# A third buffer for the split probabilities, and the magnitude sums written into the second query tile

## The chip, the cores and the metric

The program runs on one core of one Trainium2 chip. Its engines work side by side, each through its own queue in order: TensorE (PE, with its weight loads as PEld), VectorE (DVE), ScalarE (ACT), GpSimd (POOL) and SyncE (SP), which here issues nearly all DMAs. The metric is the device time of one execution in microseconds (us); less is better.

## The reference

Three parts follow one another. Inputs and output are float32.

```
scores = q @ k.T / sqrt(64)               # 4 batches x 8 heads, 576 tokens, 64 wide
kth    = 32nd largest of each row
attn   = softmax(where(scores >= kth, scores, -1e9))
x      = (attn @ v)                       # as 2304 tokens x 512
h      = x @ w_in;  x = softplus(h) @ w_out               # 512 -> 2048 -> 512
expert = argmax(x @ w_gate)               # 8 experts, one for each token
out    = gate * (relu(x @ w1[expert]) @ w2[expert])       # 512 -> 1024 -> 512
```

## The kernel before, in words

**Pairs.** Two heads of a batch make a pair; there are 16 (`m` = 0 to 15), four for each batch. For a pair, `prep_load` loads q, k and v into the raw tiles `qn`, `kn`, `vn` (pool `raw`, one buffer each, so that the next pair's load waits until this pair's tile has been read). `prep_split` cuts each number into two float16 halves: ACT writes the high half (lines 362 and 375), POOL the rest (363, 376; DVE for the first pair). Transposing DMAs bring k into `kt` (line 365) and q into `q1` (368), two plain DMAs copy q1 with its halves changed into `q2` (369, 370), and v goes to `v16`. The pool `kv`, which holds q1, q2, kt and v16, has four buffers: pair m writes where pair m-4 was.

**Magnitude sums.** `magnitudes` lets ACT take the absolute values of qn, kn and vn and keep only the sums of the rows, which a later check reads; the values themselves go to a scratch tile (`junk`, pool `stg`, one buffer) that nobody reads. For the first pair it is called at the end of `prep_split`, for the others at the end of `prep_load`.

**Groups.** The score tiles go in 72 groups of two. For a group, PE makes the scores in two pieces (line 401), which ACT copies from PSUM (lines 411 and 447). DVE finds the 32 largest of each row (lines 441 to 467). Then for both tiles ACT applies the threshold (477), POOL subtracts (478), ACT takes the exponential (479). Last, ACT writes the high half of the probabilities into `p16` (line 487), POOL the rest in two pieces (488, 489), and SP issues a DMA that transposes p16 into `pT` (491). The pool `row` gives p16 two buffers, so that the copy of line 487 waits for the transpose of the second tile before it. `e` has three buffers, pT six. The products with v (506, 508) follow three groups later. The trace gives p16 as `p`.

**The rest.** When all groups of a tile of tokens are done, it becomes a part of a unit of 256 tokens for the first layer pair (`layer1` at line 593, `layer2` at 633); the steps are emitted between the groups, 1.7 for each. After a unit come the gate and the place of each token (`route`), the row is written (698), and POOL issues an indirect DMA that scatters the tokens' numbers into a table in DRAM (701). Units 9 and 10 run behind the attention, and from about 861 us on the experts of `part_two` (lines 894 to 978).

**Order.** The program is written as a sequence with priorities. A planner puts it in order for each engine by estimated times and by when a buffer is free; on the chip each engine then runs its list in order and waits at semaphores. The branch in which `flags` is None repeats the work in another way when the check fails; with these inputs it isn't run.

Of the kernel before, what the change touches and what calls it, by code (L numbers as in the profile page):

```python
# [10 lines left out]
F16 = mybir.dt.float16  # L11
# [8 lines left out]
B, H, S, D = 4, 8, 576, 64  # L20
NT, DM, DFF = 2304, 512, 2048
E, F2 = 8, 1024
R = 9
# [38 lines left out]
LATEJ = 1  # L62
DVS = 1
C = 512
LAG = 3
SCALE = 1
ZFILL = 1
LATE = ((2, 8), (3, 0))
# [128 lines left out]
def part_one(tc, ctx, q, k, v, w_in, w_out, const, ident, before, ones, iota_e, reg_e, wg, ids,  # L197
# [8 lines left out]
    row = pool("row", 2)  # L206
    raw = pool("raw", RB)
    stg = pool("stg", 1)
# [107 lines left out]
    def prep_load(m):  # L316
        b, hp = pairs[m]
        src = []
        bd = sm.tile([128, 3], F32, name="bd") if flags is None else sums[:, m]
        for i, x in enumerate((q, k, v)):  # L320
            t = raw.tile([128, R * D], F32, name="qkv"[i] + "n")
            nc.sync.dma_start(t, x[b, 2 * hp:2 * hp + 2].rearrange("h (p r) d -> (h p) (r d)", r=R))
            src.append(t)
        pair[m] = (src, bd)
        if flags is None or m >= LATEJ:
            magnitudes(m)

    def magnitudes(m):
        src, bd = pair[m]
        junk = stg.tile([128, R * D], F16, name="junk")  # L330
        for i, t in enumerate(src):
            nc.scalar.activation(junk, t, AF.Abs, accum_out=bd[:, i:i + 1])

# [16 lines left out]
    def prep_split(m):  # L350
        qn, kn, vn, sc = pair[m] if flags is None else (*pair[m][0], None)
        sub = nc.vector if m < DVS else nc.gpsimd
        q1 = kv.tile([128, 2, R, D], F16, name="q1")
        q2 = kv.tile([128, 2, R, D], F16, name="q2")
        kt = kv.tile([128, R, 128], F16, name="kt")
        for i, xs in enumerate((kn, qn)):
            xv = xs.rearrange("p (r d) -> p r d", d=D)
            if i and m < ST0:
                st = row.tile([128, R, 2, D], F16, name="p16")
            else:  # L360
                st = stg.tile([128, R, 2, D], F16, name="st")
            nc.scalar.activation(st[:, :, 0, :], xv, AF.Copy)
            sub.tensor_tensor(out=st[:, :, 1, :], in0=xv, in1=st[:, :, 0, :], op=ALU.subtract)
            if i == 0:
                nc.sync.dma_start_transpose(out=kt, in_=st.rearrange("p r s d -> p (r s d)"))
            else:
                for h in range(2):
                    nc.sync.dma_start_transpose(out=q1[:, h], in_=st[64 * h:64 * h + 64].rearrange("p r s d -> p (r s d)"))
        nc.sync.dma_start(q2[0:64], q1[64:128])
        nc.sync.dma_start(q2[64:128], q1[0:64])  # L370

        v16 = kv.tile([128, 2, 5, 2 * D + 2], F16, name="v16")
        vs = stg.tile([128, R, 2 * D + 2], F16, name="vs")
        xv = vn.rearrange("p (r d) -> p r d", d=D)
        nc.scalar.activation(vs[:, :, 0:D], xv, AF.Copy)
        sub.tensor_tensor(out=vs[:, :, D + 2:], in0=xv, in1=vs[:, :, 0:D], op=ALU.subtract)
        nc.gpsimd.memset(vs[:, :, D:D + 2], 1.0)
        for h in range(2):
            src = vs[64 * h:64 * h + 64]
            nc.sync.dma_start(v16[0:64, h], src[:, 0:R:2])  # L380
            nc.sync.dma_start(v16[64:128, h, 0:4], src[:, 1:R:2])
            nc.sync.dma_start(v16[64:128, h, 4], src[:, 8])
        if flags is not None and m < LATEJ:
            magnitudes(m)
        pair[m] = (q1, q2, kt, v16, sc)

    sc_t, pt_t, o_t, x_t = {}, {}, {}, {}
# [31 lines left out]
    def emit_softmax(gi):  # L419
        group = groups[gi]  # L420
        n = range(2)
        s2, ps = sc_t.pop(gi)
        s = [s2[:, i] for i in n]
        sc = [pair[g[0]][4] for g in group]
        flb = 1 if flags is None else FLB
        if gi % flb == 0:
            tops[0] = sm.tile([128, 2 * flb, 32], F32, name="mx", bufs=2)
        mx = tops[0][:, 2 * (gi % flb):2 * (gi % flb) + 2]
        kth = mx[:, :, 31:32]
        e = [row.tile([128, S], F32, name="e", bufs=3) for _ in n]  # L430
        bt = sm.tile([128, 2, 1], F32, name="bias")
        if flags is None:
            src = list(s)
            wk = [row.tile([128, S], F32, name="wk") for _ in n]
        else:


            gl = ps[:, :, PS + US:PS + US + QS]
            gh = row.tile([128, 2, QS], F32, name="gt", bufs=1)
            w2 = row.tile([128, 2, S], F32, name="wk", bufs=WKB)  # L440
            nc.vector.tensor_tensor(out=gl, in0=ps[:, :, :QS], in1=s2[:, :, :QS], op=ALU.max)  # L441
            nc.vector.tensor_tensor(out=gh, in0=ps[:, :, QS:PS], in1=s2[:, :, QS:PS], op=ALU.max)
            nc.vector.tensor_tensor(out=w2[:, :, :QS], in0=gl, in1=gh, op=ALU.max)
            nc.vector.tensor_tensor(out=w2[:, :, QS:PS], in0=gl, in1=gh, op=ALU.min)
            nc.vector.tensor_copy(w2[:, :, PS:PS + US], ps[:, :, PS:PS + US])
            nc.vector.tensor_tensor(out=w2[:, :, PS + US:], in0=ps[:, :, :PS], in1=s2[:, :, :PS], op=ALU.min)
            nc.scalar.activation(s2[:, :, PS:], ps[:, :, :PS + US], AF.Copy)  # L447
            src = [w2[:, i, :QS] for i in n]
            wide = (QS, QS, PS + US, S)
        for i in n:  # L450
            nc.vector.max(out=mx[:, i, 0:8], in_=src[i])
        if flags is not None:
            nc.scalar.activation(bt, mx[:, :, 0:1], AF.Copy, scale=-SCORE, bias=LN_ESC)
        else:
            for i in n:
                nc.vector.tensor_scalar(bt[:, i], mx[:, i, 0:1], sc[i][:, 4:5], LN_ESC, op0=ALU.mult, op1=ALU.add)
        if flags is None:
            for i in n:
                nc.scalar.activation(e[i], s[i], AF.Exp, bias=bt[:, i], scale=sc[i][:, 3:4])
        for j in range(3):  # L460
            for i in n:
                to = wk[i] if flags is None else src[i]
                nc.vector.match_replace(out=to, in_to_replace=mx[:, i, 8 * j:8 * j + 8], in_values=src[i],  # L463
                                        imm_value=NEG)
                src[i] = to if flags is None else w2[:, i, :wide[j + 1]]
            for i in n:
                nc.vector.max(out=mx[:, i, 8 * j + 8:8 * j + 16], in_=src[i])  # L467
        if flags is not None and gi % FLB == FLB - 1:
            g0 = 2 * (gi - FLB + 1)
            nc.vector.tensor_tensor(out=flags[:, g0:g0 + 2 * FLB],  # L470
                                    in0=tops[0][:, :, 31:32].to_broadcast([128, 2 * FLB, 2]),
                                    in1=tops[0][:, :, 15:24:8], op=ALU.is_gt)
        for i in n:
            if flags is not None:
                if i == 0:
                    nc.scalar.activation(kths[:, 2 * gi:2 * gi + 2], kth, AF.Copy, scale=K_UP)
                nc.scalar.activation(e[i], s[i], AF.Relu, bias=kths[:, 2 * gi + i], scale=-K_UP)  # L477
                nc.gpsimd.tensor_tensor(out=e[i], in0=s[i], in1=e[i], op=ALU.subtract)  # L478
                nc.scalar.activation(e[i], e[i], AF.Exp, bias=bt[:, i], scale=SCORE)  # L479
                continue  # L480
            mk = row.tile([128, S], F16, name="mk")
            nc.vector.tensor_scalar(mk, s[i], kth[:, i], None, op0=ALU.is_ge)
            nc.gpsimd.tensor_tensor(out=e[i], in0=e[i], in1=mk, op=ALU.mult)
        for i in n:

            p16 = row.tile([128, R, 2, D], F16, name="p16").rearrange("p r s d -> p (r s d)")
            nc.scalar.activation(p16[:, 0:S], e[i], AF.Copy)  # L487
            nc.gpsimd.tensor_tensor(out=p16[:, S:S + D], in0=e[i][:, S - D:], in1=p16[:, S - D:S], op=ALU.subtract)  # L488
            nc.gpsimd.tensor_tensor(out=p16[:, S + D:], in0=e[i][:, 0:S - D], in1=p16[:, 0:S - D], op=ALU.subtract)  # L489
            pT = row.tile([128, R, 128], F16, name="pT", bufs=2 * LAG)  # L490
            nc.sync.dma_start_transpose(out=pT, in_=p16)
            pt_t[group[i]] = pT
# [272 lines left out]
    for b, hp, ts in visits:  # L765
# [3 lines left out]
        m = len(pairs) - 1 - pairs[::-1].index((b, hp))  # L769
# [17 lines left out]
    credit, started = 0, 0  # L787
    for i in range(-1, n + LAG):
        if i == -1:
# [22 lines left out]
        if 0 <= i < n:  # L812
            with tc.high_priority(offset=AHEAD):
                emit_softmax(i)
            with tc.high_priority(offset=0):
                decode_some(DECR)
        j = i - LAG
        if j >= 0:
# [283 lines left out]
```

## Time and profile before

| | us |
|---|---|
| median of 3 runs | 1096.41 (1095.99 to 1100.68) |
| profiled execution, its own time | 1104.11 |
| its span, first to last instruction | 1102.3 |
| PE busy | 900.3 (82% of the span) |
| DVE busy | 852.6 (77%) |
| ACT busy | 833.1 (76%) |
| POOL busy | 603.8 (55%) |

Busy times are sums over the span. The stages differ: attention with the first layer pair up to about 752 us, the last units up to about 861, then the experts. The profiled execution is one execution; its own time stands beside its span because the durations of the rows are those of this execution.

### The profile page before, as it was taken

To read this page: it belongs to the slowest core of one execution; us is meant where nothing else is said; L and a number is where in the kernel's file an instruction comes from. 1 tells how busy PE (TensorE), PEld (TensorE's weight loads), DVE (VectorE), ACT (ScalarE), POOL (GpSimd) and SP (SyncE) were. 2 spreads that over 40 slices of the span, in tenths; PEclk is the share of its full clock that TensorE was granted. 3 is DMA by queue.
4 is the path that set the end of the run, shared out by engine and by line. 5 is a ranking of instruction groups with operands and counts; after the bars stand their busy time and mean duration, and the time that the engine had idled before them with its cause. 6 is when DMAs were issued, how large, how long until landed. Compare 5 with 4: busy or idle time off the path is not lost.

```text
span 1102.3 us, 22261 instructions
## 1 busy us (share of the span) xinstructions
PE 900.3 (82%) x7146; PEld 664.0 (60%) x7146; DVE 852.6 (77%) x2921; ACT 833.1 (76%) x2026; POOL 603.8 (55%) x631
## 2 busy tenths in 40 slices
PE   1124359675978978799989799998999999999995
PEld 0012246344655655666556566666688899999993
DVE  3898999699966847889889799982445897777774
ACT  4889899798868867989897898994478655555553
POOL 2788898798656756767776877773101011211111
PEclk9976569876988989899999999999999999999998
DMA  7888898776756878867978646644601486676660
GB/s 173 202 200 182 180 205 180 164 159 129 126 77 122 143 122 119 134 76 126 139 153 124 106 79 93 86 80 67 202 1 30 99 252 205 217 245 227 228 222 23
DMA packets 295860, 156.98 MB, mean 142 GB/s; under 512 B 257524, under 2 KB 257652, under 8 KB 295732
## 3 DMA queue, kind: packets, MB, share of 16 engines
q1 hardware_dynamic: 292116, 145.73, 63.1%
q0 software_dynamic: 3616, 9.72, 2.6%
q8 instruction: 58, 0.95, 0.4%
q14 instruction: 70, 0.57, 0.2%
HBM read 77.89 MB, written 11.11 MB: 81 GB/s over the span
## 4 chain that ended last, share of the span: by engine, by line
PE 37%; DMA 19%; ACT 17%; POOL 9%; DVE 8%; issue 5%; SPq 3%; POOLq 0%; ACTq 0%; DVEq 0%
PE h L933 9%; DMA pT<-p 9%; PE y L946 9%; PE h L593 6%; PE y L633 4%; POOL p L489 3%; PE y L630 3%; ACT p L487 3%; POOL e L478 2%; DMA w<-in_moe_w_out_dram 2%; ACT e L479 2%; ACT e L477 2%; DVE mx L467 2%; DMA vn<-in_v_dram 2%; DVE wk L463 1%
## 5 line engine op out<-in xcount | busy, mean ns | idle before, releaser
L593 PE MATMUL h<-xT,w_in_s 128*128 128x256 f16 (+1 forms) x1920 | 231.8, 272 | 18.6 <-DMA xT<-xh 7.4
L633 PE MATMUL y<-w_out_s,g 128*128 128x512 f32 x480 | 233.9, 610 | 2.0 <-ACT g L608 2.0
L593 PEld LDWEIGHTS <-w_in_s 128*128 128x128 f16 x1920 | 177.0, 102 | 86.4 <-issue 53.8
L478 POOL TENSOR_TENSOR e<-s,e 128x576 f32<-128x576 f32 x144 | 204.0, 1432 | 22.1 <-ACT e L477 21.8
L467 DVE MAX8 mx<-wk 128x8 f32<-128x128 f32 (+2 forms) x432 | 201.1, 500 | 0.1
L401 PEld LDWEIGHTS <-q 128*128 128x128 f16 (+1 forms) x640 | 56.2, 109 | 195.7 <-issue 148.5
L489 POOL TENSOR_TENSOR p<-e,p 128x512 f16<-128x512 f32 x144 | 167.3, 1162 | 0.0
L463 DVE MATCH_REPLACE8 wk<-mx,wk 128x128 f32<-128x128 f32 (+1 forms) x432 | 144.4, 340 | 0.0
L487 ACT ACTIVATE p<-e 128x576 f16<-128x576 f32 x144 | 97.9, 683 | 42.1 <-DMA pT<-p 41.3
L401 PE MATMUL sa<-kt,q 128*128 128x256 f16 (+1 forms) x320 | 52.9, 304 | 86.7 <-ACT s L411 35.2
L633 PEld LDWEIGHTS y<-w_out_s,g 128*128 128x128 f32 x480 | 83.4, 194 | 62.4 <-issue 57.4
L913 POOL DMA_INDIRECT out_dram<-ot,idx x19 | 19.6, 1030 | 176.3 <-DVE ot L912 156.5
L479 ACT ACTIVATE e<-e,bias 128x576 f32<-128x576 f32 x144 | 111.0, 772 | 6.1 <-POOL e L478 5.9
L401 PE MATMUL sb<-kt,q 128*128 128x320 f16 (+1 forms) x320 | 63.6, 342 | 63.4 <-ACT s L447 63.4
L933 PEld LDWEIGHTS h<-xT,wf 128*128 128x128 f32 x864 | 111.9, 191 | 5.3 <-ACT wf L894 0.2
L933 PE MATMUL h<-xT,wf 128*128 128x256 f32 x864 | 114.0, 283 | 0.0
L946 PE MATMUL y<-wf,hT 128*128 128x512 f32 x432 | 112.9, 399 | 0.3 <-DVE ds L690 0.3
L477 ACT ACTIVATE e<-s,kths 128x576 f32<-128x576 f32 x144 | 106.2, 770 | 1.2 <-POOL p L489 0.4
L506 PE MATMUL m<-v,pT 128*128 128x65 f16 (+1 forms) x1440 | 96.0, 203 | 8.1 <-ACT xtail L534 6.8
L488 POOL TENSOR_TENSOR p<-e,p 128x64 f16<-128x64 f32 x144 | 45.6, 317 | 96.4 <-ACT p L487 80.9
L506 PEld LDWEIGHTS <-pT 128*128 128x128 f16 (+1 forms) x1440 | 89.5, 107 | 14.2 <-issue 10.9
L441 DVE TENSOR_TENSOR sb<-sb,s 128x256 f32<-128x256 f32 x72 | 30.6, 425 | 73.0 <-ACT s L411 48.9
(204 smaller groups left out, 1885.5 us busy)
## 6 DMA issues: line engine op xcount, KB each, us to landing
w1r<-in_moe_w_dram SPq DMA_DIRECT2D x20, 1024.0 KB, 6.0
w2r<-in_moe_w_dram SPq DMA_DIRECT2D x20, 1024.0 KB, 7.7
w<-in_moe_w_in_dram SPq DMA_DIRECT2D x16, 512.0 KB, 5.1
w<-in_moe_w_out_dram SPq DMA_DIRECT2D x16, 512.0 KB, 4.2
rows<-xr SPq DMA_DIRECT2D x37, 128.2 KB, 2.4
qn<-in_q_dram SPq DMA_DIRECT2D x16, 288.0 KB, 3.4
kn<-in_k_dram SPq DMA_DIRECT2D x16, 288.0 KB, 3.2
vn<-in_v_dram SPq DMA_DIRECT2D x16, 288.0 KB, 3.7
```

Source lines behind the costliest of these rows:

```text
L401: last_qk[0] = nc.tensor.matmul(ps[p0:p1], lhsT=qs[:, h, r0:r1, :].rearrange("p r d -> p (r d)"), rhs=kt[:, k0:k1, cs], start=first, stop= ...
L463: nc.vector.match_replace(out=to, in_to_replace=mx[:, i, 8 * j:8 * j + 8], in_values=src[i], imm_value=NEG)
L467: nc.vector.max(out=mx[:, i, 8 * j + 8:8 * j + 16], in_=src[i])
L478: nc.gpsimd.tensor_tensor(out=e[i], in0=s[i], in1=e[i], op=ALU.subtract)
L479: nc.scalar.activation(e[i], e[i], AF.Exp, bias=bt[:, i], scale=SCORE)
L487: nc.scalar.activation(p16[:, 0:S], e[i], AF.Copy)
L489: nc.gpsimd.tensor_tensor(out=p16[:, S + D:], in0=e[i][:, 0:S - D], in1=p16[:, 0:S - D], op=ALU.subtract)
L506: nc.tensor.matmul(o[:, h, 0:D + 1], lhsT=pT(r), rhs=v16[:, h, c, 0:D + 1], start=r == 0, stop=r == R - 1)
L593: nc.tensor.matmul(hps[:, :n], lhsT=w_in_s[:, c, j, p, o:o + 128], rhs=xT[:, 0:len(u.tiles), r, c, :], start=m == 0, stop=m == 3 * KD - 1)
L633: nc.tensor.matmul(u.y[i], lhsT=g[:, cs], rhs=w_out_s[:, f, :], start=f == 0, stop=f == KF - 1)
L933: nc.tensor.matmul(h, lhsT=w1f[:, a, c, :], rhs=xT[:, b, c, :], start=n == 0, stop=n == 3 * KD - 1)
L946: nc.tensor.matmul(y[i], lhsT=hT[g][:, a, i * 128:i * 128 + 128], rhs=w2f[:, b, :], start=g == 0 and n == 0, stop=g == KF2 - 1 and n == 2)
```

## The change

p16 gets three buffers in the branch that runs (`PB = 3`) and keeps two in the other. The scratch tile `junk` is gone. `magnitudes` is given the place to write: for the pairs after the first it is called in `prep_split`, once q1, q2 and kt are allocated and before the first split, and writes into one half of q2, which the two DMAs of lines 369 and 370 fill afterwards; for the first pair it is called where it was and writes into a p16 buffer. In the branch that isn't run, the sums write into a buffer `st`, and the mask `mk` has one buffer in place of two.

```diff
+PB = 3
...
         pair[m] = (src, bd)
-        if flags is None or m >= LATEJ:
-            magnitudes(m)
-
-    def magnitudes(m):
+        if flags is None:
+            magnitudes(m, stg.tile([128, R * D], F16, name="st"))
+
+    def magnitudes(m, junk):
         src, bd = pair[m]
-        junk = stg.tile([128, R * D], F16, name="junk")
         for i, t in enumerate(src):
             nc.scalar.activation(junk, t, AF.Abs, accum_out=bd[:, i:i + 1])
...
         kt = kv.tile([128, R, 128], F16, name="kt")
+        if flags is not None and m >= LATEJ:
+            magnitudes(m, q2[:, 0].rearrange("p r d -> p (r d)"))
         for i, xs in enumerate((kn, qn)):
             xv = xs.rearrange("p (r d) -> p r d", d=D)
             if i and m < ST0:
-                st = row.tile([128, R, 2, D], F16, name="p16")
+                st = row.tile([128, R, 2, D], F16, name="p16", bufs=PB if flags is not None else 2)
...
         if flags is not None and m < LATEJ:
-            magnitudes(m)
+            magnitudes(m, row.tile([128, R, 2, D], F16, name="p16", bufs=PB if flags is not None else 2).rearrange("p r s d -> p (r s d)")[:, :R * D])
...
-            mk = row.tile([128, S], F16, name="mk")
+            mk = row.tile([128, S], F16, name="mk", bufs=1)
...
-            p16 = row.tile([128, R, 2, D], F16, name="p16").rearrange("p r s d -> p (r s d)")
+            p16 = row.tile([128, R, 2, D], F16, name="p16", bufs=PB if flags is not None else 2).rearrange("p r s d -> p (r s d)")
```

## Rows read from the trace of the kernel before

**Rows 1.** Stretches: us, then busy PE, PEld, DVE, ACT, POOL, clock, DMA, GB/s.

```profile
200.00:490.00 290.00, 233.13 (x1960) 156.38 (x1960) 229.67 (x876) 237.90 (x599) 206.88 (x216) 0.86 0.73 125
490.00:752.00 262.00, 245.08 (x2200) 165.18 (x2199) 227.60 (x903) 230.18 (x587) 192.48 (x205) 1.00 0.68 109
752.00:861.00 109.00, 107.25 (x823) 81.78 (x822) 54.15 (x243) 70.29 (x219) 11.32 (x13) 1.00 0.25 69
```

**Rows 2.** Waits up to 752 us: who waited for whom, us in total, times, longest.

```profile
ACT p L487 <- DMA pT<-p: 41.3, 19, 8.0
```

**Rows 3.** The scatter's line up to 752 us: durations in ns, landing in us.

```profile
L701 POOL DMA_INDIRECT table<-ids,dsti x12: 984/992/1152, 294.7 to 744.7; - x12
...
DMA to landing us min/median/max: 7.2/9.1/13.5
```

**Rows 4.** Timeline of POOL: start, us, instruction.

```profile
410.12 1.00 POOL L701 DMA_INDIRECT table<-ids,dsti  x1 [0.15 <-issue]
```

**Rows 5.** The chain that ended last, near 410 us: start, us, what.

```profile
410.39 10.91 DMA pT<-p
```

**Rows 6.** Line 487 around its four longest waits: first and last start; ACT's idle time.

```profile
L487 ACT ACTIVATE p<-e x2: 677/680/682, 308.4 to 313.1; 128x576 f16<-128x576 f32 x2
...
  DMA pT<-p: 8.0, 1
...
L487 ACT ACTIVATE p<-e x2: 682/687/692, 334.2 to 338.4; 128x576 f16<-128x576 f32 x2
...
  DMA pT<-p: 4.5, 1
...
L487 ACT ACTIVATE p<-e x2: 682/686/691, 421.4 to 424.8; 128x576 f16<-128x576 f32 x2
...
  DMA pT<-p: 5.7, 1
...
L487 ACT ACTIVATE p<-e x2: 666/674/683, 605.0 to 607.0; 128x576 f16<-128x576 f32 x2
...
  DMA pT<-p: 3.7, 1
```

**Rows 7.** ACT's waits: in 200 to 300 us, 300 to 490 (two), 490 to 752.

```profile
ACT p L487 <- DMA pT<-p: 3.5, 4, 1.5
...
ACT p L487 <- DMA pT<-p: 21.6, 5, 8.0
ACT junk L332 <- DMA vn<-in_v_dram: 6.8, 2, 6.6
...
ACT p L487 <- DMA pT<-p: 16.3, 10, 3.7
```

**Rows 8.** PE's waits for ACT's copies in 300 to 490 us.

```profile
PE sa L401 <- ACT s L411: 12.9, 5, 6.7
PE h L667 <- ACT x2T L663: 6.1, 1, 6.1
PE sb L401 <- ACT s L447: 3.0, 2, 2.8
```

**Rows 9.** PE's longest wait in 490 to 752 us.

```profile
PE sa L401 <- ACT s L411: 5.7, 5, 3.2
```

**Rows 10.** Timeline of PE behind ACT's wait for a v load.

```profile
396.58 0.80 PE L401 MATMUL sa<-kt,q 128*128 128x256 f16 x3 [6.68 <-ACT s L411]
```

**Rows 11.** Timelines of ACT and SP: one sum for q, one transpose into kt.

```profile
398.54 0.68 ACT L332 ACTIVATE junk<-qn 128x576 f16<-128x576 f32 x1
...
406.46 1.30 SPq L365 DMA_TRANSPOSE kt<-st  x1
```

**Rows 12.** SP's waits for PE before the transpose into kt, up to 752 us.

```profile
SPq L365 <- PE m L506: 11.9, 4, 4.7
...
SPq L365 <- PE sa L401: 0.6, 1, 0.6
```

**Rows 13.** The score matmuls from 100 us on: idle before them, times.

```profile
  ACT s L447: 45.9, 14
```

## The prediction

> **What bounds the kernel now.** I read the table of stretches first. To about 752 us attention and the first layer pair run together; there ACT is 82 to 88% busy and PE 80% from 200 to 490 us (at a granted clock of 0.86 in the mean, between its two levels), then 94% from 490 to 752 at 1.00; from 752 on PE has 98% and nothing that is edited runs [rows 1]. So the change can act only before 752 us, most of it before 490, where PE still has 57 us without work. Every later PE instruction keeps its place behind these, so a us that PE saves there comes off the end.
>
> Next the list of waits: up to 752 us ACT stood 41.3 us, in 19 waits, before the copy of the probabilities into p16 (line 487), for the transposing DMA that still reads the buffer [rows 2]. Why is that DMA late? Each routed tile sends an indirect scatter into the table; there are 12 before 752 us, which land after a median of 9.1 us [rows 3]. One starts at 410.12 [rows 4], and the transpose issued at 410.39 lands 10.91 us later [rows 5], when the scatter is through. With two p16 buffers ACT, whose queue is in order, then stops, and the scores' copies for PE (lines 411, 447) stand behind the stopped copy.
>
> **The third buffer.** Copy k waits for the transpose of copy k-3 instead of k-2. The four longest waits are 8.0, 4.5, 5.7 and 3.7 us, and the copy after each starts 4.7, 4.2, 3.4 and 2.0 us later [rows 6]. The stopped copy goes through, since the transpose three before had landed earlier; but the following copy now waits for the very landing that stopped its predecessor, so the wait less that distance remains: 3.3, 0.3, 2.3 and 1.7, together 7.6. The other 15 waits are shorter than their distance and go. Of 41.3 us ACT keeps 7.6 and is free of 33.7.
>
> What is late next is PE's own work, or DVE's. By stretch:
> - 200 to 300 us: ACT waits 3.5 for p16 [rows 7], all cleared. The decoding of the weights fills its queue here, so the value lies between 0 and 3.5; I take 1.0, near the low end since ACT is rarely the one that waits.
> - 300 to 490: ACT waits 21.6 [rows 7], of which 3.3 + 0.3 + 2.3 = 5.9 stay, so 73% goes. PE waited here for ACT's copies 12.9 + 6.1 + 3.0 = 22.0 us [rows 8]. Of these 6.7 follow another stop, of a magnitude sum for a v load [rows 10], and stay. 15.3 x 0.73 = 11.1 us. Ends: 0 (all of it turns into waits for DVE), and 15.7 (every us of ACT reaches the end). I take 11.1, as PE's own rows are the nearest.
> - 490 to 752: ACT waits 16.3 [rows 7] and keeps 1.7. PE is nearly full; its longest wait for ACT is 5.7 in sum [rows 9]. 5.7 x 14.6 / 16.3 = 5.1; I take half, 2.5, because work that PE gets earlier here queues behind PE's other work. Ends 0 and 14.6.
>
> [...]
>
> **The sums into q2.** As many activations of the same shape run as before; nothing is added on ACT. Emission moves them from the load of a pair to its split, behind the allocation of q1, q2 and kt. Which wait is new? A sum writes a q2 buffer that the matmuls of the pair four before still read. Before, the sum for q ran at 398.54 and the transpose into the same pair's kt, which needs the same release, was issued at 406.46 [rows 11]; so sums will start some 8 us later there. Two costs follow.
> - The raw tiles are held longer, so SP issues the next pair's loads later, with the splits and transposes behind them. Cover: from 100 us on PE's waits before its score matmuls are for ACT or issue, with no DMA of kt or q among them; the longest that names an engine is ACT's line 447 [rows 13]. I cost it at nothing; were that cover gone, every pair could lose PE a wait like that of [rows 10], 6.7.
> - ACT itself may reach a sum before PE has let q2 go. Behind it stand the scores' copies and the exponentials, and PE and DVE wait for these. SP waits for that release before kt: 11.9 us in four waits down to 0.6 in one, five lines, ten waits, 20.7 in all [rows 12]. So the price lies between 0 and 20.7 x 15.3 / 21.6 = 14.7 us of PE (the rate at which ACT's stops reached PE above). I take 3, near the low end: SP arrives early because it has little else to do, ACT arrives late because it is 82% busy.
>
> The first pair's sum, moved to a p16 buffer, stays in the first microseconds beside the loads: 0. The load wait of 6.8 [rows 7] is neither removed nor aimed at, since a v load still comes only after the v tile before has been split; the planner sets each engine's order anew and such a stop may go or come once: 0, ends -6.7 and +6.7. The one-buffer mask belongs to the branch that doesn't run.
>
> Sum: -1.0 - 11.1 - 2.5 + 3 = -11.6 us. The profiled execution took 1104.11 us (span 1102.3, 1.8 around it), 7.7 above the median of the three timed runs. 1104.11 - 11.6 = 1092.5; taken off the median, 1096.41 - 11.6 = 1084.8 us.
>
> **Rivals.**
> - *The wait is moved, not removed.* ACT runs on, fills e and the SP queue, and PE or DVE ends the same steps as before. For it: PE is at 94% after 490 us, and DVE at 87%. Against: before 490 PE waits for just those ACT copies [rows 8]. About -2: 1094 us.
> - *ACT stops for q2 (slower).* One mechanism: the sum stands in ACT's order ahead of PE's release, in each of the 12 pairs from the fifth on. Break-even is at 14.6 / 0.71 = 20.6 us, or 1.7 us for a pair. SP's ten waits average 2.1 and the longest is 4.7 [rows 12]; at 3.4, between them, 12 x 3.4 x 0.71 = 29.0, less 14.6: +14.4, 1111 us. For it: in the row of before the sum runs 8 us ahead of the release. Against: the planner knows of the release and can place ACT's other work first.
> - *All of ACT's time comes through*, PE included, with the higher clock of a PE that is not let idle: -33.7 + 3 = -30.7, 1066 us. For it: the clock of 0.86 before 490 us against 1.00 after [rows 1]. Against: PE's 94%.
> - *The third buffer is no use* because consecutive transposes all land behind one scatter: then the 7.6 left over would be nearer 41, about -1 + 3: 1098. It falls together with the first rival in outcome; by the distances of [rows 6] a scatter of 9.1 us covers two or three copies, which speaks against it.
>
> **How the numbers follow.** The forecast 0.47 (own range 1077 to 1090); moved, with the useless buffer, 0.27; all of it 0.12; slower 0.14. A measurement here can tell 0.5%, 5.5 us, from no change. Forecast and large gain are faster: 0.59; moved: 0.27; slower: 0.14. The range 1069 to 1099 holds the forecast, the moved wait and a part of the large gain, and leaves out most of the slower case.
>
> **What would show it.** ACT's wait before line 487 for the transposes falls from 41.3 to about 8 us, the rest of it at second copies inside scatters; PE's wait for lines 411, 447 and 663 between 300 and the end of the fourth unit falls by about 11; the sums in the trace move to just behind the last score matmul of the pair four before, with ACT waits for PE at their line of some us in all; attention ends near 740 us, and the parts behind it keep their lengths. It is wrong if p16's waits go and attention still ends at 750 (moved), if ACT's line of the sums waits over 20 us for PE (slower), or if the wait at line 487 stays above 20.

## The result and the profile after

The changed kernel took 1062.2 us in the median of four runs (1054.09 to 1067.08), the kernel before 1098.55 (1095.99 to 1103.68): a ratio of 0.966, 95% interval 0.9622 to 0.9698, or 36 us less. I had forecast 11.6 us less and a range down to 1069. The direction was right, the size a third.

The profiled execution of after was the shortest of its four (1054.09, span 1052.3), that of before, 1104.11, was above every timed run of it here. So the two traces lie 50 us apart, and the medians 36. From the traces I take where the time went, from the ratios how much.

The page of after: busy times, the granted clock in 40 slices, and the chain that ended last.

```profile
PE 883.3 (84%) x7146; PEld 655.5 (62%) x7146; DVE 849.6 (81%) x2921; ACT 831.5 (79%) x2026; POOL 603.1 (57%) x631
...
PEclk9976669867999999999999999999999999999998
...
PE 42%; DVE 11%; ACT 4%; DMA 3%; issue 3%; POOL 2%; SPq 1%; POOLq 0%; ACTq 0%; DVEq 0%
```

The chain of before:

```profile
PE 37%; DMA 19%; ACT 17%; POOL 9%; DVE 8%; issue 5%; SPq 3%; POOLq 0%; ACTq 0%; DVEq 0%
```

DMA and ACT are nearly gone from it. But PE's busy time fell as well, from 900.3 to 883.3 us, for the same 7146 matmuls. The granted clock of both traces stands at two levels, 1.00 and 0.50 of full speed (before: 1.00 from 343 to 393 us, 0.50 from 101 to 137). In stretches at the lower one, where the first layer's matmuls start 213 ns apart in the median instead of 109, lay 92.9 us of PE's busy time up to unit 9 before and 60.9 after. If the lower level doubles a matmul, half of the difference, 16.0 us, is by this estimate what the clock gave of the 16.8 by which that busy time fell.

Now the stages, bounded by the same steps of the program in each kernel: the first DVE instruction of groups 12, 24, 36 and of the last group, PE's first matmul of unit 9, and its first of the experts. Each row has the stretch, its length, busy time and count of PE, PEld, DVE, ACT and POOL, the granted clock, the DMA share and GB/s. First before:

```profile
0.00:154.00 154.00, 44.06 (x372) 28.27 (x373) 123.50 (x384) 121.80 (x259) 116.89 (x127) 0.76 0.84 190
154.00:284.30 130.30, 99.13 (x797) 63.94 (x796) 117.13 (x373) 116.82 (x279) 109.07 (x107) 0.84 0.74 156
284.30:424.30 140.00, 121.68 (x969) 81.00 (x966) 97.20 (x397) 104.00 (x268) 86.30 (x91) 0.91 0.74 120
424.30:731.60 307.30, 282.59 (x2564) 191.94 (x2564) 277.45 (x1093) 274.57 (x710) 227.39 (x244) 0.97 0.70 111
731.60:782.60 51.00, 48.08 (x408) 32.89 (x407) 25.64 (x170) 27.42 (x82) 21.42 (x24) 1.00 0.44 92
782.60:863.80 81.20, 80.18 (x621) 63.37 (x619) 40.37 (x130) 59.54 (x181) 6.05 (x6) 1.00 0.21 60
863.80:1102.30 238.50, 224.59 (x1430) 202.54 (x1428) 171.36 (x380) 128.95 (x253) 36.69 (x35) 0.98 0.61 197
```

And after:

```profile
0.00:143.20 143.20, 40.03 (x368) 26.11 (x368) 118.00 (x383) 118.09 (x246) 112.51 (x122) 0.81 0.87 195
143.20:271.00 127.80, 98.58 (x793) 64.18 (x790) 118.47 (x376) 119.80 (x287) 113.80 (x113) 0.83 0.75 165
271.00:389.70 118.70, 110.05 (x946) 74.00 (x943) 97.77 (x394) 101.50 (x261) 82.41 (x87) 0.97 0.86 141
389.70:693.70 304.00, 291.24 (x2652) 198.75 (x2651) 276.96 (x1103) 280.03 (x733) 231.79 (x248) 0.99 0.66 115
693.70:733.50 39.80, 38.86 (x354) 26.42 (x353) 26.24 (x161) 23.77 (x69) 19.94 (x23) 1.00 0.67 105
733.50:814.50 81.00, 79.98 (x622) 63.37 (x620) 40.74 (x133) 59.50 (x181) 5.83 (x6) 1.00 0.22 65
814.50:1052.30 237.80, 224.54 (x1430) 202.64 (x1428) 171.38 (x380) 128.78 (x253) 36.85 (x35) 0.98 0.59 198
```

All of it lies ahead of unit 9, which starts at 733.5 instead of 782.6; unit 9 and the experts keep their lengths to 1 us, as forecast. The largest piece is the third stage (groups 24 to 36), where the scatters begin: 21.3 us. The first gives 10.8, the fifth 11.2, in part because 54 of its matmuls now stand ahead of it. Over the five stages PE was idle 187.1 us before and 154.7 after (lengths less busy times), 32.3 less, and busy 16.8 less; together the 49.1 by which unit 9 moved.

ACT's waits in 271 to 455 us (total, times, longest), and the page's group of the copy into p16 (busy, mean ns of one, idle before it and what ended most of that):

```profile
ACT st L364 <- DMA q<-st: 5.9, 3, 3.2
ACT p L489 <- DMA pT<-p: 4.0, 1, 4.0
```

```profile
L489 ACT ACTIVATE p<-e 128x576 f16<-128x576 f32 x144 | 97.5, 683 | 4.5 <-DMA pT<-p 4.0
```

Of the 41.3 us of [rows 2] 4.0 is left, in one wait. The scatters have not become faster: up to unit 9 they land as in [rows 3], where the three values are 7.2, 9.1 and 13.5.

```profile
L703 POOL DMA_INDIRECT table<-ids,dsti x13: 982/987/1149, 280.7 to 713.3; - x13
...
DMA to landing us min/median/max: 7.1/8.4/13.9
```

PE's waits in 271 to 455 us:

```profile
PE h L595 <- ACT sa L609: 4.9, 4, 3.3
...
PE sb L403 <- ACT s L449: 2.9, 2, 2.0
...
PE h L669 <- ACT x2T L665: 1.5, 1, 1.5
PE sa L403 <- ACT s L413: 0.7, 1, 0.7
```

The 12.9, 6.1 and 3.0 of [rows 8] have become 0.7, 1.5 and 2.9; a wait of 4.9 for the first layer's ACT work is new at the top. From 455 to 704 the 5.7 of [rows 9] is 2.9.

Last, the sums, ACT's times and then all that they waited for:

```profile
L332 ACT ACTIVATE q<-qn x15: 666/672/687, 13.9 to 543.5; 128x576 f16<-128x576 f32 x15
...
  DMA qn<-in_q_dram: 2.9, 2
  DMA vn<-in_v_dram: 1.4, 2
  DMA kn<-in_k_dram: 0.5, 1
```

No wait for PE stands there. The stop of 6.8 for a v load [rows 7] is 1.4 in the whole span.

### The profile page after: what moved, and what is told of

Read it like the earlier page. It is cut to its first block, busy times and chain, and to the rows that moved or that the text cites. A ratio compares the mean times of both kernels' runs of the same rounds, so it can differ in the third digit from the quotient of the medians.

```text
span 1052.3 us, 22312 instructions
## 1 busy us (share of the span) xinstructions
PE 883.3 (84%) x7146; PEld 655.5 (62%) x7146; DVE 849.6 (81%) x2921; ACT 831.5 (79%) x2026; POOL 603.1 (57%) x631
## 4 chain that ended last, share of the span: by engine, by line
PE 42%; DVE 11%; ACT 4%; DMA 3%; issue 3%; POOL 2%; SPq 1%; POOLq 0%; ACTq 0%; DVEq 0%
PE h L935 10%; PE y L948 10%; PE h L595 7%; PE y L635 6%; PE y L632 3%; DVE mx L469 3%; DVE wk L465 3%; DMA q<-st 1%; DMA xT<-xh 1%; PE m L508 1%; DVE wk L448 1%; PE tp L905 1%; PE h L669 1%; PE sb L403 1%; POOL e L480 1%
## 5 line engine op out<-in xcount | busy, mean ns | idle before, releaser
L595 PE MATMUL h<-xT,w_in_s 128*128 128x256 f16 (+1 forms) x1920 | 228.4, 269 | 16.4 <-ACT sa L609 9.5
L635 PE MATMUL y<-w_out_s,g 128*128 128x512 f32 x480 | 230.0, 602 | 5.0 <-ACT g L610 5.0
L595 PEld LDWEIGHTS <-w_in_s 128*128 128x128 f16 x1920 | 174.5, 101 | 79.8 <-issue 51.2
L403 PE MATMUL sb<-kt,q 128*128 128x320 f16 (+1 forms) x320 | 61.2, 333 | 61.7 <-ACT s L449 61.6
L508 PE MATMUL m<-v,pT 128*128 128x65 f16 (+1 forms) x1440 | 93.8, 202 | 1.3 <-ACT xtail L536 0.8
L508 PEld LDWEIGHTS <-pT 128*128 128x128 f16 (+1 forms) x1440 | 87.2, 106 | 11.2 <-issue 7.2
L948 PEld LDWEIGHTS y<-wf,hT 128*128 128x128 f32 x432 | 76.7, 189 | 13.4 <-DVE ds L692 0.3
```

Source lines behind the costliest of these rows:

```text
L403: last_qk[0] = nc.tensor.matmul(ps[p0:p1], lhsT=qs[:, h, r0:r1, :].rearrange("p r d -> p (r d)"), rhs=kt[:, k0:k1, cs], start=first, stop= ...
L508: nc.tensor.matmul(o[:, h, 0:D + 1], lhsT=pT(r), rhs=v16[:, h, c, 0:D + 1], start=r == 0, stop=r == R - 1)
L595: nc.tensor.matmul(hps[:, :n], lhsT=w_in_s[:, c, j, p, o:o + 128], rhs=xT[:, 0:len(u.tiles), r, c, :], start=m == 0, stop=m == 3 * KD - 1)
L635: nc.tensor.matmul(u.y[i], lhsT=g[:, cs], rhs=w_out_s[:, f, :], start=f == 0, stop=f == KF - 1)
L948: nc.tensor.matmul(y[i], lhsT=hT[g][:, a, i * 128:i * 128 + 128], rhs=w2f[:, b, :], start=g == 0 and n == 0, stop=g == KF2 - 1 and n == 2)
```

## The experiments

Ratios are against the kernel before, run beside each on the same chip.

### Each part alone

**e1_sums_only**: after, with two p16 buffers.

```diff
-PB = 3
+PB = 2
```

> The change with PB = 2: the sums go into q2, p16 keeps two buffers. Theory A (the third buffer does it: ACT no longer stops behind a transpose that waits for a scatter): about 1096 to 1100 us, no gain; ACT's wait for p16 stays near 41 us. Theory B (the planner's new order does it, since attention is 10 us ahead by group 12, where line 487 never waited for p16): 1085 us or less, and the first 150 us as short as in the changed kernel. Theory C (slower rival of the prediction: ACT stops at the sums for q2): 1104 us or more.

1087.79 us, ratio 0.9889 (0.9853 to 0.9925): 12 us faster, where the prediction had 3 us slower. From its trace ACT's wait before p16, its page's busy times, and the third stage:

```profile
ACT p L489 <- DMA pT<-p: 39.9, 22, 11.3
```

```profile
PE 889.4 (82%) x7146; PEld 657.6 (60%) x7146; DVE 847.8 (78%) x2921; ACT 832.3 (76%) x2026; POOL 603.0 (55%) x631
```

```profile
276.50:400.10 123.60, 110.34 (x952) 74.35 (x949) 100.13 (x401) 102.84 (x265) 84.05 (x91) 0.96 0.76 133
```

The p16 stops are all still there. Its profiled span is 12.9 us shorter (1089.4 for 1102.3), and 10.9 of that is PE's busy time, 889.4 for 900.3: PE was idle as long as before (200.0 us for 202.0), but its matmuls were shorter, at a clock of 0.96 for 0.91 in this stage. That holds for this one execution. Over the whole span its granted clock was 0.932; in e1's other five runs it was 0.921 to 0.927, no higher than in the runs of before beside them (0.917 to 0.937, median 0.925), and they took 1081 to 1091 us, no longer than this one. So it is not shown that the 12 us are a gain of the clock.

**e2_third_buffer_only**: before, with three p16 buffers; the sums keep scratch and place. Room comes from the zero row, now a view of another tile, and the one-buffer mask.

```diff
-    zrow = const.tile([27, 19], F32, name="zrow")
...
+    zrow = kths[0:27, 0:19, 0]
...
-            p16 = row.tile([128, R, 2, D], F16, name="p16").rearrange("p r s d -> p (r s d)")
+            p16 = row.tile([128, R, 2, D], F16, name="p16", bufs=PB if flags is not None else 2).rearrange("p r s d -> p (r s d)")
```

> The kernel before with a third p16 buffer and nothing else moved: the sums stay at the load and write into their scratch tile (the 96 bytes that this lacks come from the zero row, which becomes a view of the thresholds' tile). Theory A: 1062 to 1072 us, most of the 36 us, ACT's wait for p16 about 5 us. Theory B: 1075 to 1090 us, and the lead of 10 us at group 12 is missing.

1069.58 us, ratio 0.9726 (0.9697 to 0.9756): 30 us from the buffer alone. Its p16 wait, and its first five stages:

```profile
ACT p L487 <- DMA pT<-p: 7.8, 4, 6.1
```

```profile
0.00:151.00 151.00, 43.04 (x378) 27.65 (x379) 118.14 (x385) 123.19 (x262) 117.84 (x126) 0.74 0.85 194
151.00:276.80 125.80, 98.64 (x790) 64.04 (x790) 114.64 (x374) 116.19 (x280) 108.97 (x109) 0.86 0.75 160
276.80:394.90 118.10, 109.86 (x936) 73.77 (x933) 98.21 (x394) 100.83 (x261) 85.07 (x90) 0.94 0.81 137
394.90:700.30 305.40, 289.17 (x2615) 197.07 (x2614) 276.93 (x1093) 275.94 (x716) 227.82 (x244) 0.98 0.75 113
700.30:747.20 46.90, 45.24 (x391) 30.66 (x389) 24.90 (x170) 26.05 (x78) 21.19 (x25) 1.00 0.46 100
```

7.8 us of the wait are left, where I had worked out 7.6; but one wait, behind the first scatter, holds 6.1 of them:

```profile
ACT p L487 <- DMA pT<-p: 6.1, 1, 6.1
```

Unit 9 starts 35.4 us earlier: PE idle 25.8 less (161.2 for 187.1), PE busy 9.6 less. The traces lie 35 us apart, the medians 30, so some 5 us of these are a matter of which execution was traced. The two ratios multiply to 0.9618, against 0.966 measured for both together: about the sum of the parts.

### The scatters left out

**e3_before_no_scatter, e4_after_no_scatter, e12_third_buffer_no_scatter** leave out the indirect DMA that writes the tokens' places into the table, in before, after and e2, so that the experts read the table's fill. The same edit in each:

```diff
-        wr = nc.gpsimd.indirect_dma_start(out=table, out_offset=bass.IndirectOffsetOnAxis(ap=dsti[:, :1], axis=0),
-                                          in_=ids[:, col:col + 1], in_offset=None)
```

> The kernel before without the indirect scatter of the tokens' numbers into the table (left out, so that the experts work on the fill row). Theory A: with nothing in the way the transposes land after 3 to 4 us; ACT's wait for p16 falls from 41 to under 12 us and the time to about 1065 to 1075 us. Theory B: the wait may fall, but the time stays within 10 us of before (1088 or more).

> The changed kernel without the same scatter. Theory A: little more to gain, 1050 to 1060 us, so that it leads the kernel before without scatters by 15 us or less. Theory B: its lead over that kernel stays near 36 us.

> The kernel before with the third p16 buffer alone and no scatter into the table (left out). The same buffer won 30 us with the scatters. Theory A (it wins by riding over the scatters): 1050 to 1058 us, that is 0 to 9 us under the 1058.9 of the kernel before without scatters. Rival (the buffer wins in any case, by the distance that it gives ACT): 1030 to 1040 us.

| | ratio | us |
|---|---|---|
| e3, before without scatters | 0.9629 (0.959 to 0.9669) | 1058.88 |
| e12, third buffer without scatters | 0.9534 (0.949 to 0.9577) | 1048.09 |
| e4, after without scatters | 0.9453 (0.9417 to 0.9488) | 1037.99 |

With scatters the third buffer is worth 30 us, without them 10 (0.9629 to 0.9534). So some 20 of its 30 are the riding over scatters. They still cost after about 23 us (0.966 to 0.9453), although its p16 stops are down to 4.0. Of the 23, 2.3 lie in the experts' stage, which reads the fill (237.8 to 235.5 us). ACT also waits 14.8 us in after for the transposes of k and q and the copies of v, and 4.2 in e4; its waits for the loads of q, k and v are no shorter in e4. The third stage of e4, at the full clock, and its stage from the last group to unit 9:

```profile
272.50:379.80 107.30, 104.90 (x943) 72.45 (x940) 96.86 (x394) 101.16 (x260) 79.59 (x84) 1.00 0.83 153
...
671.00:718.50 47.50, 47.50 (x402) 32.11 (x402) 25.46 (x173) 27.50 (x81) 19.66 (x23) 1.00 0.44 98
```

The third stage is 11.4 us shorter than in after, with PE idle 2.4 us instead of 8.7 and 5.2 us less busy for three matmuls fewer.

### The scatters later

**e5_after_late_scatter** and **e6_before_late_scatter** keep the places of ten tiles in SBUF and issue their scatters once the last group's thresholds are there, in after and in before; the other eight go by themselves.

```diff
+        held = flags is not None and not flushed
+        if held:
+            nc.vector.tensor_copy(places_f[:, len(places):len(places) + 1], dst)
...
+        if i == n and flags is not None:
+            z = sm.tile([128, 1], F32, name="zlast", bufs=1)
+            nc.vector.tensor_scalar(z, kths[:, 2 * n - 1], 0.0, None, op0=ALU.mult)
+            nc.vector.tensor_scalar(places_i[:, :len(places)], places_f[:, :len(places)], z, None, op0=ALU.add)
+            for x, (col, after) in enumerate(places):
+                scatter(places_i[:, x:x + 1], col, after, x == len(places) - 1)
```

> The changed kernel with the scatters of the attention stage held: their places are kept in SBUF and the indirect DMAs issued once the last group's thresholds are there, so that none stands among the transposes. Theory A (a scatter in flight keeps every later transpose and load from being reported as landed): 1036 to 1048 us, near the 1038 of the kernel without scatters. Rival (the held scatters delay the first experts' reads of the table): 1055 us or more, with PE idle before the experts.

> The kernel before with the scatters held in the same way, two p16 buffers. Theory A: 1056 to 1068 us, near the 1059 of the kernel before without scatters, and ACT's wait for p16 under 15 us. Rival: above 1080 us.

Before gained: 1075.27, ratio 0.9779 (0.9758 to 0.9801). After didn't: 1059.84, ratio 0.9652 (0.9632 to 0.9673), against 0.966. Its third stage was down to 106.3 us, but the scatters now came in a bunch between the last transposes, and the stage from the last group to unit 9 was 59.0 us, where e4 needs 47.5 for as many matmuls (402; after has 354 there, in 39.8 us). PE was idle 7.4 in it, and the clock fell to 0.91:

```profile
677.20:736.20 59.00, 51.57 (x403) 34.48 (x401) 24.93 (x171) 25.12 (x74) 29.60 (x33) 0.91 0.47 87
```

**e9_after_later_scatter**, **e13_after_scatter_held**, **e15_after_scatters_behind** and **e17_scatters_behind_whole** hold 13 of them until unit 9; e13 and e15 issue the earlier tiles' scatters first. In the first three part of the experts' work ran on the table's fill: the first experts start to read the table at 712 to 714 us, ahead of the held scatters, which start at 734 to 736. The traces of all three hold 18 scatters, as many as that of before; that e9 and e13 lose a tile, as the expectation of e15 says, isn't seen there. In e17 the experts' first places depend on a read of the table that comes behind them, and the computation is whole.

```diff
+            if u.number == 9 and f == 4:
+                release(e_sums[:, k:k + 1])
...
+        back = sm.tile([128, 1], I32, name="back", bufs=1)
+        nc.sync.dma_start(back, table[0:128, :])
+        nc.vector.tensor_scalar(z, back, 0.0, None, op0=ALU.mult)
+        nc.vector.tensor_scalar(early, early, z, None, op0=ALU.add)
```

The first two lines are those of e9, e13 and e15, the others are e17's.

> The changed kernel with the scatters held as in the run before, but let go only when the ninth unit's fifth step has its sums, that is after the last transposes of the attention and of the units. In the earlier run the held scatters all stood together among the last transposes, and the stage from the last group to the ninth unit took 59.0 us in place of 39.8 to 47.4. Theory A (a scatter in flight holds back every transpose): 1038 to 1046 us, that stage 46 to 48 us. Rival (the experts' first reads now wait for the scatters): 1052 us or more, with PE idle just before the experts.

> The changed kernel with the scatters held until the ninth unit's fifth step, in an order in which the experts' first reads wait for all the scatters that they need (in the run before they did not wait, so its 1042 us hold an experts' stage on the fill row for some tokens). Theory A: the attention stage is as without scatters, and the reads find the scatters landed: 1038 to 1048 us. Rival (the reads wait): 1052 us or more, with PE idle before the experts.

> The changed kernel with all scatters up to the eighth unit held until the ninth unit's fifth step, none lost (the two runs before let go of all but the tile whose place was known when they were released). Theory A: 1039 to 1048 us, as with that tile missing, and faster than both kernels. Rival: above 1052 us.

> The changed kernel with the 13 scatters of the first seven units held until the ninth unit has begun, and the experts' first places made to depend on a read of the table behind them, so that the first experts work on the right rows (in the runs before their reads ran 20 us ahead of the held scatters). Theory A: 1039 to 1050 us, 12 to 23 us under the changed kernel. Rival (the experts' weights queue behind the read on SP and come late): above 1055 us, with PE idle before and in the first expert.

Ratios: e9 0.9486 (0.9451 to 0.952), e13 0.9501 (0.9473 to 0.9528), e15 0.949 (0.9455 to 0.9526), e17 0.9703 (0.9674 to 0.9733) at 1067.32 us. In e17 unit 9 starts at 723.4, ten us before that of after, but the table is read from 771.6 us on, in after from 727.0, and the stretch to the experts takes 104.8 us instead of 81.0, PE idle 17.0 in it (6.2 of that before the first expert's rows) and at a clock of 0.89:

```profile
723.40:828.20 104.80, 87.78 (x622) 68.25 (x620) 42.36 (x139) 60.05 (x181) 21.70 (x21) 0.89 0.23 63
```

So the 1042 us of the other three were bought with reads that didn't wait. In the two whole versions, e5 and e17, what the attention stage gains is given back behind it. I found none faster than after.

### The place of the sums

**e7_sums_place_only**: after with two p16 buffers, the sums at the split but into a scratch tile of their own. **e10_first_sums_at_split**, **e11_later_sums_at_split**: before, with only the sums of the second to fourth pair, or only the later ones, moved to the split.

```diff
-            magnitudes(m, q2[:, 0].rearrange("p r d -> p (r d)"))
+            magnitudes(m, stg.tile([128, R * D], F16, name="junk"))
```

```diff
-        if flags is None or m >= LATEJ:
+        if flags is None or (m >= LATEJ and m >= KVB):
             magnitudes(m)
...
+        if flags is not None and m >= LATEJ and m < KVB:
+            magnitudes(m)
```

The second diff is e10; e11 has the two comparisons with KVB the other way round.

> The sums emitted in the split, as in the change, but into a scratch tile of their own, with two p16 buffers: the place without the q2 buffer. Theory D (the 12 us of the sums alone come from the order that the planner makes of the new place): 1085 to 1092 us. Theory E (they come from the wait for q2, which holds sums and loads back until the pair four before is done): 1096 to 1102 us.

> The kernel before, with only the sums of the first four pairs emitted in the split (scratch tile, two p16 buffers). Theory I (what the place brings is won in the first 150 us, where the first pairs are prepared): group 12 starts 7 us earlier, as in the run with all sums moved, and the time is 1087 to 1094 us. Theory J (it is won later, by sums and loads of the later pairs): 1096 to 1101 us, group 12 as before.

> The complement: only the sums of the fifth to the last pair are emitted in the split. Theory I: 1096 to 1101 us and group 12 as before. Theory J: 1087 to 1094 us.

e7 0.9941 (0.992 to 0.9961), e10 0.9981 (0.9955 to 1.0007), e11 0.9973 (0.9945 to 1.0002). The place alone gives some 6 of e1's 12 us; the rest would be q2 as the target, though the intervals of e1 and e7 touch. Neither e10 nor e11 can be told from no change. In e10 group 12 starts at 147.2 instead of 154.0 (143.2 in after, 151.3 in e11), so most of the early lead of after comes from the first pairs, but it is not kept.

### More and less work on ACT

**e8_act_load** emits 13 small ACT copies with each of 13 routed tiles. **e14_no_later_sums** leaves the sums of all pairs after the first out of after (45 activations with their read-outs), with a constant in place of the sums that the check reads; **e16_no_sums_no_scatter** does the same in e4.

```diff
+            for _ in range(13):
+                nc.scalar.activation(iota_i.bitcast(F32), iota_e, AF.Copy)
```

```diff
+        if flags is not None and m >= LATEJ:
+            nc.vector.memset(bd, 100.0)
+            return
```

> The changed kernel with 13 tiny copies of about 0.2 us on ACT added at each of 13 routed tiles before the attention ends: 34 us of ACT time, as much as the third buffer freed, put back where the scatters are. Theory F (a us of ACT costs nearly a us of the end): 1088 to 1096 us. Theory G (0.43 of it, as the prediction had it, since PE is nearly full): 1073 to 1080 us. Theory H (ACT has slack, the waits mattered for what they held up, not for their time): under 1070 us.

> The changed kernel without the magnitude sums of the second to the last pair (left out, a constant in their place): 45 activations of 0.68 us and 45 reads of the sum of 0.19 us less on ACT, 39 us. Theory G (a us of planned ACT work is worth about half a us at the end, as the 34 us put in cost 17): 1040 to 1046 us. Theory F (a us for a us, as the stops were): 1022 to 1030 us. Theory H (nothing): 1056 us or more.

> The changed kernel without the sums of the second to the last pair and without the scatters (both left out). Leaving out the sums alone made the changed kernel 12 us slower, with ACT's wait for p16 back at 19.9 us. Theory K (less ACT work brings ACT to the copies sooner, and the scatters turn that into stops): without scatters the 39 us of work are worth something again, 1015 to 1034 us against 1038. Theory L (the planner's order for the shorter work is bad by itself): 1044 us or more.

e8: 1078.93 us, ratio 0.9813 (0.979 to 0.9837), 17 us more than after. The group of the added copies, the page's busy times and the p16 wait:

```profile
L701 ACT ACTIVATE iota_i<-iota_e 128x8 f32<-128x8 f32 x169 | 34.3, 203 | 0.8
```

```profile
PE 897.9 (83%) x7146; PEld 662.3 (61%) x7146; DVE 849.8 (79%) x2921; ACT 848.8 (79%) x2195; POOL 603.1 (56%) x631
```

```profile
ACT p L489 <- DMA pT<-p: 12.0, 6, 7.3
```

Two things differ from what the experiment meant to do. The copies' 34.3 us overlap with the instructions beside them: ACT's busy time rose by 17.3 us only, from 831.5 to 848.8. And the copies read nothing of their tile, so the planner set them early: they start between 2.1 and 277.1 us, and the first scatter starts at 289.8. So e8 puts no work where the scatters are, and its 17 us answer 17 us of ACT work; its stops for p16 are 8.0 us longer as well. The range of theory G was met, but not for its reason.

e14: 1074.45 us, ratio 0.9782 (0.9753 to 0.9811). With 28 us less on ACT (busy 803.5 for 831.5; the 39 us of the expectation are the sum of overlapping durations) it is 12 us slower than after. Its waits up to 760 us:

```profile
ACT p L492 <- DMA pT<-p: 19.9, 5, 7.2
ACT vs L380 <- DMA v<-vs: 11.9, 4, 6.7
ACT st L367 <- DMA kt<-st: 10.9, 6, 3.2
```

The planner put every engine's work in another order, and in that order ACT meets the held landings again. e16 has no scatters and is still slower than e4: 1047.68 us, ratio 0.9554 (0.9507 to 0.9601) for 0.9453. There more of the first layer's steps were left behind the last group:

```profile
668.10:727.10 59.00, 57.64 (x457) 38.69 (x455) 26.25 (x172) 30.92 (x92) 18.35 (x22) 1.00 0.41 85
```

457 matmuls stand in that stage, 402 in that of e4, which takes 47.5 us. So less work on ACT came with some 10 us more, twice. That the planner's new order does this fits both traces, but no run changes the order alone.

## Why the prediction was wrong

**The freed wait: right in its sum.** I had 33.7 of 41.3 us going and 7.6 staying, by the distances of [rows 6]. With the buffer alone 7.8 stayed (e2), with both parts 4.0. That 7.6 and 7.8 agree so well is luck. I had each stopped copy go through and the next one wait, 3.3 us at most. In e2 the 50th copy, which waited 8.0 before, still waits 6.1: with the first scatter the transpose three before it was held too. The other three waits are 1.7 together. In after the 50th copy goes through and the 51st waits 4.0, as I had it. With PE's idle time and the whole falling as they did, the rival of the moved wait falls, and so does that of the useless buffer, which came up at one scatter only, e2's first.

**What it is worth to PE: mis-sized, the failing step.** My terms -1.0 - 11.1 - 2.5 = -14.6 measured -30 us (e2). I had turned ACT's freed time into PE's time by those PE waits alone that name one of ACT's copies, and left PE's busy time as it was. To compare term by term I bound the stretches by the steps next to 200, 300 and 490 us of before, the first maximum (MAX8) of groups 16, 26 and 43, and end with unit 9. Before, then e2:

```profile
204.30:303.50 99.20, 71.50 (x597) 46.79 (x595) 88.91 (x312) 84.34 (x196) 80.94 (x83) 0.82 0.73 143
303.50:489.10 185.60, 158.32 (x1343) 107.41 (x1343) 137.51 (x555) 148.38 (x390) 123.38 (x131) 0.89 0.73 115
489.10:782.60 293.50, 274.83 (x2422) 185.30 (x2421) 243.92 (x1029) 243.25 (x631) 198.81 (x213) 1.00 0.64 107
```

```profile
201.90:295.60 93.70, 67.08 (x594) 45.61 (x595) 86.13 (x310) 81.13 (x191) 76.59 (x80) 0.84 0.76 147
295.60:460.10 164.50, 151.56 (x1345) 103.86 (x1345) 138.16 (x556) 146.05 (x389) 123.14 (x131) 0.93 0.80 134
460.10:747.20 287.10, 274.41 (x2409) 184.62 (x2408) 243.83 (x1029) 243.08 (x630) 198.32 (x213) 0.99 0.69 108
```

- *The clock was not in the sum.* PE's busy time up to unit 9 fell by 9.6 us, 6.8 of them in the middle stretch, where I had held it constant. In stretches at the lower level lay 92.9 us of PE's busy time before and 76.1 in e2; half of the difference, 8.4, is by the estimate above what the clock gave. In e2's other five runs the clock over the span is 0.932 to 0.937, against a median of 0.925 in before. I had read the 0.86 of [rows 1] and used it only for the large rival.
- *Idle time was counted too narrowly.* It fell by 1.1 us in the first of these stretches, where I had 1.0, by 14.3 in the middle one for my 11.1, and by 6.0 in the last for my 2.5, which I had halved. Another 4.4 went ahead of them, where by [rows 2] and [rows 7] p16 has no stop; what took them is open.

For the last stretch I had the ends 0 and 14.6. It lost 6.4 in e2, 6.0 of it idle time by matmuls, and 17.7 in after, with both parts and 32 matmuls fewer there, 12.5 of it idle time. That PE is full by its matmuls, as the 2.5 took it, e4 bears out: in its stage from the last group to unit 9 PE has no idle time by matmuls, 47.50 busy of 47.50 us, while its weight loads take 32.11.

**The conversion rate itself.** I priced ACT time by what PE had waited, 14.6 / 33.7, or 0.43 for each us. The runs have 0.7 to 1.0: 33.5 us of stops removed brought 30 (before to e2, 0.9), 35.9 brought 25 (e1 to after, 0.7), 11.7 without scatters brought 10 (e3 to e12, 13.9 to 2.2 us, 0.9), and 17.3 us of work put in cost 17 (e8, 1.0, its longer stops included). So the rate was too low with scatters and without, and for work as for stops. Only taking 28 us of work out doesn't follow it: that cost 12 (e14).

**The sums into q2: wrong in sign.** I had +3 for waits of ACT for PE. There are none in after, and e1 is 12 us faster. The slower rival, 1111 us, falls: its condition, that the sum stands ahead of PE's release, did not come up: ACT reached every sum after that release (in e8, with a fuller ACT, one such wait of 0.8 us appears). What the gain is made of, I can't settle: some 6 for the place, the rest with q2 as the target (e7). In e1's trace nearly all of it is shorter busy time of PE, but the clocks of its other runs don't bear that out. A part may be a chance of the planner's order, which no run changes alone.

**The rivals.** The nearest was that all of ACT's time comes through, with the higher clock, 1066 us. I gave it 0.12 because PE stood at 94%. That share holds for the stretch from 490 us, and 29.0 of e2's 35.4 us lay ahead of it. That 1066 is near the 1062.2 of after is part luck: it has the whole 33.7 us of ACT's time for the buffer, which gave 30, and 3 lost by the sums, which gave 12.

**The signs.** p16's wait fell as said, PE's waits for lines 411, 447 and 663 fell by 17 of their 22 us rather than 11, the later parts kept their lengths. The sign for the sums (waits for PE at their line) did not show, and unit 9 came 49 us earlier, not 12.

## What to carry to other kernels

Where stops go in a stretch in which TensorE's clock stands between its levels in the mean (0.91 in the third stage of before), add to the idle time that goes what its own matmuls gain at the higher level (those of the first layer start 109 ns apart there instead of 213); here PE's busy time was a third of the movement in the trace of after, 16.8 of 49.1 us. Price a wait for a DMA by everything that stands behind the same landing, and find the transfer that holds it: leaving the scatters out was worth 41 us before the change (3 of them in the experts' stage), and a deeper buffer got half of what they cost. Where a planner sets the order anew, measure each part of a change alone, and look where the added work stands in the trace before you price it.

## What was not expected of the hardware

An indirect DMA of 128 numbers, 7.1 to 13.9 us from issue to landing, held back the transposes issued behind it on another queue: without scatters the third buffer's p16 waits are 2.2 us (e12) instead of 7.8, before's 13.9 (e3) instead of 41.3. While a scatter was under way, SP issued 19 DMAs in before and 21 in after whose landing the trace tells, 23 of them transposes; all 40 landed after that scatter, the nearest 0.17 us after it. The transpose of [rows 5] is one of them: the scatter of [rows 4] lands 10.6 us after its issue, at 420.7, and the transpose at 421.3; in the median of that trace a transpose into pT lands 3.5 us after its issue. How the scatter holds them back is not shown.

The same 7146 matmuls took 900.3 us of PE's busy time before, 890.3 in e2, 883.3 in after and 876.5 in e4. Nothing in them was edited. Between the ends lie 24 us, and the granted clock of the third stage went from 0.91 to 1.00 beside them.
